# Cross attention followed by a maxout layer on one core: batch 0, W2·Wo and batch 1's attention in another written order

## The chip, the cores and the metric

One core of a Trainium2 chip runs the whole kernel. The metric is device time in microseconds (us) of one execution, the median of several. Engines: PE (TensorE, matrix products), DVE (VectorE), ACT (ScalarE), POOL (GpSimd) and SP (SyncE), which here issues all transfers.

## The reference

For each of 8 batches and 8 heads, `x` (512 tokens by 64) and a small `state` (32 by 64) attend to each other. The outputs, 544 rows a batch with the 8 heads side by side (512 columns), go through a layer that takes the maximum of two products.

```python
scores  = x @ state.T / 8;   a  = softmax(scores);   xread = a @ state     # 512 rows
scores2 = state @ x.T / 8;   a2 = softmax(scores2);  sread = a2 @ x        # 32 rows
h = concatenate([xread, sread])              # (8*544, 512)
out = maximum(h @ w1, h @ w2) @ w_out        # w1, w2: 512x1024, w_out: 1024x512
```

## The kernel before, in words

The maximum is rewritten: max(h w1, h w2) w_out = relu(h (w1 − w2)) w_out + h (w2 w_out). So the kernel needs `wd` = w1 − w2, `wo` = w_out in bf16 and `wwo` = w2·w_out, the last computed on PE (`w_wo`, line 422): 32 products of 512 columns from the transposed w2 (`w2t`, made in `w2_tr`, line 407) and `wo`. The weights come in four quarters of the 1024 hidden columns; each quarter is three transfers of 512 KB (`load_wq`, line 97) into staging tiles of which three of a kind exist.

For a batch `b`, xread = a·state is never formed. `sw` (line 304) multiplies `state` into the weights instead: SW[b] = state·wd (1024 columns) and state·wwo (512 columns). Layer 1 (`l1`, line 347) is relu(a·SW) in 8 pieces of two products, written to `r`. Layer 2 (`l2`, line 370) adds, for each of 4 tiles of 128 tokens, a·state·wwo (`l2_open`, line 356, two products from `aT`) and r·wo (`l2_f`, line 360, eight products). The attention of a batch is: cast x to bf16 (`xb`), transpose it (`xt`), scores and exp (`e`), row sums and division (`norm`, line 229, result `a`), transpose `a` (`aT`). The state's own read (`sread_mm`, line 256, called "the state read" below) multiplies `e` with x and, for the sums, with ones; from batch 2 on x and ones stand together in a tile `xo` of its own (`cast_x1`, line 144). Its result is scaled on DVE (`sread_norm`) and transposed (`sread_tr`); the 256 state rows of all batches go through the two layers at the end (`moe_sread`).

PSUM has eight banks, in two pools of four: `ps` for short products and `pa` (tile name `acc`) for layer 2 and the last chunk of `sw`. A pool hands its banks out in turn, so a product waits for the copy that empties the bank used four requests before.

The order of the work on each engine is the order in which the program is written (line 48, a manual schedule). Lines 446 to 555 are the first part: loads, batch 0, the four quarters of the weights, and the attention of batch 1. Batch 0 runs layer 2 in quarters as `wo` arrives (`l2_part`, line 439), keeping four `pa` banks open. Lines 558 to 590 are a loop over batches 1 to 7: layer 1, scores and division of the next batch, then the four tiles of layer 2 with `sw_all` and the state read of the next batch behind the second. `idle` (line 433) issues products on zeros. All transfers are on SP's one queue and are served in their order. Lines 58, 60 and 62 are the copy helpers on ACT, DVE and POOL.

Of the kernel before, what the change touches and what calls it, by code (L numbers as in the profile page):

```python
# [15 lines left out]
def kernel(  # L16
# [92 lines left out]
    def state0():  # L109
        nc.vector.tensor_copy(sb0, sf0)  # L110
# [5 lines left out]
        nc.vector.tensor_scalar(sbdn, sbd[:, 0], scalar1=-1.0, scalar2=None, op0=ALU.mult)  # L116
# [9 lines left out]
    def states():  # L126
        p = bank(BF16)
        for m in range(8):
            nc.tensor.transpose(p[:, m * 128:(m + 1) * 128], sbr[:, m].rearrange("p j d -> p (j d)"), ident)
        for j, e in ((0, "A"), (1, "V")):  # L130
            o = sbd[64 * j:64 * j + 64, 1:B, :, 32 * j:32 * j + 32].rearrange("p b k (l m) -> p (b k) l m", l=4)
            i = p[64 * j:64 * j + 64, :].rearrange("p (m k l) -> p k l m", m=8, l=4)[:, 4:]
            copy(e, o, i)


    def cast_x(b, engs):
        xb = xio.tile([128, NC, H * D], BF16, tag="xb", name="xb")
        for g in range(2):
            copy(engs[g],
                 xb[:, :, 256 * g:256 * g + 256].rearrange("p c (i d) -> p i c d", i=4),  # L140
                 xf_t[b][:, 4 * g:4 * g + 4, :].rearrange("p i (c d) -> p i c d", c=NC))
        st[b] = dict(xb=xb)

    def cast_x1(b):

        xo = stage.tile([128, NC, H, 66], BF16, tag="w1f", bufs=3, name="xo")
        nc.gpsimd.memset(xo[:, :, :, 64:65], 1.0)
        for g in range(2):
            nc.gpsimd.tensor_copy(xo[:, :, 4 * g:4 * g + 4, 0:D].rearrange("p c i d -> p i c d"),  # L149
                                  xf_t[b][:, 4 * g:4 * g + 4, :].rearrange("p i (c d) -> p i c d", c=NC))  # L150
        st[b]["xo"] = xo

    def cast_pair(b, k, eng):
        if k == 0:
            st[b] = dict(xb=xio.tile([128, NC, H * D], BF16, tag="xb", name="xb"))
        copy(eng, st[b]["xb"][:, :, 128 * k:128 * k + 128].rearrange("p c (i d) -> p i c d", i=2),
             xf_t[b][:, 2 * k:2 * k + 2, :].rearrange("p i (c d) -> p i c d", c=NC))

    def xt_pair(b, k, eng):
# [4 lines left out]
        for c in range(NC):  # L164
            nc.tensor.transpose(p[:, c * 128:(c + 1) * 128], d["xb"][:, c, k * 128:k * 128 + 128], ident)
# [48 lines left out]
    def scores(b, hh, pool=None):
        d = st[b]
        if hh == 0:
            att_tiles(b)
        p = bank(F32, pool)
# [6 lines left out]
        ev = d["e"].rearrange("p g c i n -> p (g c) i n")[:, :, 2 * hh:2 * hh + 2, :]  # L225
        nc.scalar.activation(out=ev.rearrange("p (g c) i n -> p g c (i n)", g=2),  # L226
                             in_=p.rearrange("p (c g m) -> p g c m", c=NC, g=2), func=ACTF.Exp, scale=scale)

    def norm(b, hh, eng):
# [16 lines left out]
    def at_pe(b, engs, pool=None):  # L246
        d = st[b]
        AT[b] = keep.tile([128, 2, NC, 128], BF16, tag="at", name="aT")
        for g in range(2):
            p = bank(BF16, pool)  # L250
            for c in range(NC):
                nc.tensor.transpose(p[:, c * 128:(c + 1) * 128],
                                    d["a"][:, g, c].rearrange("p i n -> p (i n)"), ident)
            copy(engs[g], AT[b][:, g].rearrange("p c t -> p (c t)"), p[:, 0:512])

    def sread_mm(b, pool=None):
# [15 lines left out]
        if "xo" not in d:
            for g in range(2):
                for c in range(NC):
                    nc.tensor.matmul(p[:, 256 + g:257 + g], d["e"][:, g, c].rearrange("p i n -> p (i n)"), ones[:, 0:1],
                                     start=False, stop=(c == NC - 1), skip_group_check=True)

    def sread_norm(b):
# [5 lines left out]
        if "xo" in d:  # L284
            pv = p[:, 0:260].rearrange("p (g i d) -> p g i d", g=2, i=2)
            nc.vector.reciprocal(rr, pv[:, :, 0, D])
            pv = pv[:, :, :, 0:D]
        else:
            nc.vector.reciprocal(rr, p[:, 256:258])
            pv = p[:, 0:256].rearrange("p (g i d) -> p g i d", g=2, i=2)  # L290
        for g in range(2):
            nc.vector.tensor_scalar(sr[:, :, g, :], pv[:, g], scalar1=rr[:, g:g + 1], scalar2=None, op0=ALU.mult)

    def sread_tr(b, eng, pool=None):
        d = st[b]
        p = bank(BF16, pool)
        for i in range(2):
            nc.tensor.transpose(p[:, i * 128:(i + 1) * 128], d["sr"][:, i].rearrange("p g d -> p (g d)"), ident)
        for i in range(2):
            copy(eng, sread_t.rearrange("p (a i) t -> p i a t", i=2)[:, i, :, b * Ns:(b + 1) * Ns],  # L300
                 p[:, i * 128:(i + 1) * 128].rearrange("p (a i n) -> p i a n", a=2, i=2)[:, i])


    def sw(b, lo, hi, engs=("V", "A"), pool=None):
        if b not in SW:
            SW[b] = big.tile([128, 2, WC], BF16, tag="sw", name="sw")
        pg = [bank(F32, pool), bank(F32, pool)]
        n = hi - lo
        for i in range(4):
            for g in range(2):  # L310
                rhs = wd[64 * g:64 * g + 64, i, lo:hi] if hi <= FF else wwo[64 * g:64 * g + 64, i, lo - FF:hi - FF]
                nc.tensor.matmul(pg[g][32 * i:32 * i + 32, 0:n],  # L312
                                 sbd[64 * g:64 * g + 64, b, i, 32 * g:32 * g + 32], rhs, start=True, stop=True)
        for g in range(2):
            copy(engs[g], SW[b][:, g, lo:hi], pg[g][:, 0:n])

    def sw_first(engs):

        SW[0] = big.tile([128, 2, WC], BF16, tag="sw", name="sw")
        pg = [bank(), bank()]  # L320
# [26 lines left out]
    def l1(b, f, eng=None):  # L347
        if f == 0:
            R[b] = big.tile([128, NF, NC * 128], BF16, tag="r", name="r")
        p = bank()  # L350
# [3 lines left out]
        relu(R[b][:, f, :], p, eng)  # L354
# [10 lines left out]
    def l2_out(b, c, p, eng):  # L365
        if c == 0:
# [36 lines left out]
    def w2_cast(q, eng):  # L403
        w2b[q] = stage.tile([128, 4, FQ], BF16, tag="w2b", bufs=2, name="w2b")
        copy(eng, w2b[q].rearrange("p i f -> p (i f)"), w2f[q].rearrange("p i f -> p (i f)"))

    def w2_tr(q, eng, pool=None):
        p = bank(BF16, pool)
# [4 lines left out]
        copy(eng, w2t[:, 2 * q:2 * q + 2].rearrange("p f i t -> p (f i t)"), p)  # L413
# [207 lines left out]
```

## Time and profile before

| | us |
|---|---|
| runs of the kernel | 165.0, 162.18, 163.86; median 163.86 |
| the profiled execution | 165.27 |
| its span, from the first to the last instruction | 163.6 |
| start of batch 1's layer 1 (end of the first part) | 50.34 |
| one batch in the loop (94.53 to 109.17) | 14.64 |

Over the span PE is busy 148.0 us, DVE 87.8, ACT 66.8 and POOL 54.6. The mean granted clock of PE is 0.986. Times in the rows are us from the span's start, unless they are marked ns. PE's "busy" counts overlapping products once, and the last product of a group shows some 0.2 us of its way through the array. PEld is the loading of weights.

### The profile page before, as it was taken

What the parts mean: (1) busy time and instruction counts of PE and PEld (TensorE: products, weight loads), DVE (VectorE), ACT (ScalarE), POOL (GpSimd) and SP (SyncE); (2) the same over time, 40 slices, a digit from 0 to 9 for tenths busy, and PEclk for the clock granted to TensorE, in tenths of its full rate; (3) what the DMA queues carried; (4) which work ended last, traced back from release to release, by engine and by line L of the source; (5) the groups of instructions that cost most, each with busy time, mean ns of one, the idle gap of its engine ahead of it and who ended that gap; (6) DMA issues with size and microseconds to landing.
All of it is one profiled execution on the core that took longest, in us unless ns stands there. A gap on an engine that the chain in (4) does not pass through costs nothing.

```text
span 163.6 us, 2847 instructions
## 1 busy us (share of the span) xinstructions
PE 148.0 (90%) x1142; PEld 71.7 (44%) x1142; DVE 87.8 (54%) x167; ACT 66.8 (41%) x131; POOL 54.6 (33%) x65
## 2 busy tenths in 40 slices
PE   5779989675999999998998999899999989999990
PEld 1436434453433544544453454345354534564430
DVE  3275756756867853654585457447554843731110
ACT  4234872544057450814454072537226451621000
POOL 1559455005940272263509225450900310000000
PEclk9999999998799999999999999999999999999998
DMA  3999999950234947798495858659523230601333
GB/s 93 271 373 360 363 360 356 353 187 2 52 76 192 196 72 251 257 132 214 170 284 101 262 212 176 146 174 311 104 38 160 96 67 1 256 0 36 98 128 128
DMA packets 34861, 29.09 MB, mean 178 GB/s; under 512 B 19872, under 2 KB 32160, under 8 KB 33952
## 3 DMA queue, kind: packets, MB, share of 16 engines
q1 hardware_dynamic: 34848, 28.91, 59.9%
q8 instruction: 9, 0.15, 0.4%
q14 instruction: 4, 0.03, 0.1%
HBM read 15.27 MB, written 8.91 MB: 148 GB/s over the span
## 4 chain that ended last, share of the span: by engine, by line
PE 71%; issue 12%; ACT 6%; DVE 3%; DMA 3%; SPq 1%; POOL 1%; POOLq 0%
PE acc L362 25%; PE ps L352 17%; PE acc L358 8%; PE ps L425 5%; DMA xf<-in_x_dram 3%; PE ps L268 2%; ACT ob L58 2%; PE ps L386 2%; PE acc L396 2%; ACT sw L58 2%; PE ps L223 2%; PE ps L411 2%; PE ps L312 1%; PE acc L394 1%; SPq L90 1%
## 5 line engine op out<-in xcount | busy, mean ns | idle before, releaser
L362 PE MATMUL acc<-wo,r 128*128 128x512 bf16 x256 | 60.5, 379 | 0.0
L362 PEld LDWEIGHTS <-r 128*128 128x128 bf16 x256 | 24.9, 98 | 29.5
L343 DVE TENSOR_SCALAR r<-ps 128x512 bf16<-128x512 f32 x32 | 22.1, 692 | 18.8 <-PE ps L352 18.7
L352 PE MATMUL ps<-aT,sw 128*128 128x512 bf16 x128 | 30.4, 387 | 1.2 <-DVE sw L60 1.2
L58 ACT COPY ob<-acc 128x512 f32<-128x512 f32 x16 | 9.4, 586 | 53.9 <-PE acc L362 36.0
L235 POOL TENSOR_TENSOR a<-e,er 128x512 bf16<-128x512 bf16 x14 | 14.4, 1051 | 47.4 <-DVE er L234 23.9
L341 ACT ACTIVATE r<-ps 128x512 bf16<-128x512 f32 x32 | 19.4, 605 | 11.2 <-PE ps L352 10.6
L62 POOL CAST xb<-xf 128x1024 bf16<-128x1024 f32 (+1 forms) x17 | 16.4, 974 | 21.3 <-DMA xf<-in_x_dram 21.2
L60 DVE COPY ob<-acc 128x512 f32<-128x512 f32 x16 | 10.7, 667 | 19.3 <-PE acc L362 18.9
L60 DVE CAST sw<-ps 128x512 bf16<-128x512 f32 (+1 forms) x20 | 12.0, 630 | 14.4 <-PE ps L312 12.9
L358 PE MATMUL acc<-sw,aT 128*128 128x512 bf16 x64 | 19.0, 380 | 0.3 <-DVE sw L60 0.3
L352 PEld LDWEIGHTS <-sw 128*128 128x128 bf16 x128 | 12.2, 98 | 15.2 <-DVE sw L60 1.4
L58 ACT CAST sw<-ps 128x512 bf16<-128x512 f32 (+1 forms) x20 | 10.3, 551 | 8.6 <-PE ps L312 7.3
L149 POOL CAST xo<-xf 128x1024 bf16<-128x1024 f32 x12 | 12.2, 1044 | 0.0
L233 DVE TENSOR_REDUCE es<-e 128x16 f32<-128x512 bf16 x14 | 9.2, 656 | 1.5 <-ACT e L226 1.5
L226 ACT ACTIVATE e<-ps 128x512 bf16<-128x512 f32 x14 | 7.6, 594 | 2.2 <-PE ps L223 1.6
L425 PE MATMUL ps<-wo,w2t 128*128 128x512 bf16 x32 | 8.3, 413 | 0.0
L358 PEld LDWEIGHTS <-aT 128*128 128x128 bf16 x64 | 5.2, 98 | 5.5 <-issue 0.9
L437 PE MATMUL acc<-wz 128*128 128x512 bf16 x13 | 6.4, 586 | 1.2 <-DVE ones L457 1.2
L268 PEld LDWEIGHTS <-e 128*64 128x64 bf16 x128 | 4.3, 116 | 5.9 <-ACT sw L58 5.5
L312 PE MATMUL ps<-wd,sbd 64*32 64x512 bf16 (+1 forms) x136 | 5.5, 364 | 1.4 <-DVE wd L416 1.4
L268 PE MATMUL ps<-xo,e 128*64 128x130 bf16 x96 | 4.0, 224 | 2.6 <-ACT sw L58 2.6
(93 smaller groups left out, 135.1 us busy)
## 6 DMA issues: line engine op xcount, KB each, us to landing
xf<-in_x_dram SPq DMA_DIRECT2D x14, 512.0 KB, 5.4
out_dram<-ob SPq DMA_DIRECT2D x7, 1024.0 KB, 4.4
w2f<-in_moe_w_dram SPq DMA_DIRECT2D x4, 512.0 KB, 9.2
w1f<-in_moe_w_dram SPq DMA_DIRECT2D x4, 512.0 KB, 9.8
wof<-in_moe_w_out_dram SPq DMA_DIRECT2D x4, 512.0 KB, 9.4
xf<-in_x_dram SPq DMA_DIRECT2D x4, 256.0 KB, 3.5
out_dram<-ob SPq DMA_DIRECT2D x2, 512.0 KB, 2.6
sfr<-in_state_dram SPq DMA_DIRECT2D x2, 256.0 KB, 8.6
```

The costliest lines, as they stand in the source:

```text
L58: nc.scalar.copy(o, i)
L60: nc.vector.tensor_copy(o, i)
L62: nc.gpsimd.tensor_copy(o, i)
L149: nc.gpsimd.tensor_copy(xo[:, :, 4 * g:4 * g + 4, 0:D].rearrange("p c i d -> p i c d"), xf_t[b][:, 4 * g:4 * g + 4, :].rearrange("p i (c d ...
L235: (nc.gpsimd if eng == "P" else nc.vector).tensor_mul(av, ev, d["er"][:, hh].unsqueeze(3).to_broadcast([128, 2 * NC, 2, Ns]))
L268: nc.tensor.matmul(p[64 * ih:64 * ih + 64, g * 2 * m:(g + 1) * 2 * m], d["e"][:, g, c, 2 * ih:2 * ih + 2].rearrange("p i n -> p (i n)"), x ...
L341: nc.scalar.activation(out=o, in_=p, func=ACTF.Relu)
L343: nc.vector.tensor_scalar(o, p, scalar1=0.0, scalar2=None, op0=ALU.max)
L352: nc.tensor.matmul(p, SW[b][:, g, f * 128:(f + 1) * 128], AT[b][:, g].rearrange("p c t -> p (c t)"), start=(g == 0), stop=(g == 1))
L358: nc.tensor.matmul(p, AT[b][:, g, c, :], SW[b][:, g, FF:WC], start=(start and g == 0), stop=(stop and g == 1))
L362: nc.tensor.matmul(p, R[b][:, f, c * 128:(c + 1) * 128], wo[:, f, :], start=(start and j == 0), stop=(stop and j == len(fs) - 1))
L425: nc.tensor.matmul(p, w2t[:, f, i, :], wo[:, f, :], start=(j == 0), stop=(j == len(fs) - 1))
```

## The change

The first part is written out anew. Its helpers are split into the products (`..._mm`) and the copy that empties the bank (`..._ev`), and 130 calls stand in a new order. W2·Wo is 16 pieces (a quarter, a block of rows) of two products; quarters 1 and 2, which shared a bank and one addition before, are now added one by one. x0 comes in two loads of 512 KB in place of four of 256 KB, the first ahead of state 0; all weights are loaded before x1. x0, and x1 too, are cast straight into the layout with ones (`xo`, now with the ones ahead of and behind each pair of heads), and the state read takes its operand from there. It takes its bank from `pa` in the loop. Some casts and differences change engine: w2's quarters 0 and 3 go from POOL to ACT, quarter 1 from ACT to POOL; w1 − w2 is on POOL for quarters 1 to 3 and on DVE for quarter 0, the reverse of before; w_out's quarter 1 goes from POOL to DVE, 2 from POOL to ACT, 3 from ACT to POOL.

```diff
+    load_x(0, 2, 0)
     load_state0()
-    load_x(0, 4)
-    for q in range(3):
-        load_wq(q)
+    load_x(0, 2, 1)
+    load_w2(0)
...
-    def cast_x1(b):
-        xo = stage.tile([128, NC, H, 66], BF16, tag="w1f", bufs=3, name="xo")
-        nc.gpsimd.memset(xo[:, :, :, 64:65], 1.0)
-        for g in range(2):
-            nc.gpsimd.tensor_copy(xo[:, :, 4 * g:4 * g + 4, 0:D].rearrange("p c i d -> p i c d"),
-                                  xf_t[b][:, 4 * g:4 * g + 4, :].rearrange("p i (c d) -> p i c d", c=NC))
+    def cast_xo(b):
+        alloc_x(b, "P", stage.tile([128, NC, 4, 132], BF16, tag="w1f", bufs=3, name="xo"))
+        for k in (0, 2):
+            cast_pair(b, k, "P", 2)
+    def alloc_x(b, eng, xo):
+        (nc.gpsimd if eng == "P" else nc.vector).memset(xo[:, :, :, 1:131:129], 1.0)
+        st.setdefault(b, {})["xo"] = xo
+    def cast_pair(b, k, eng, m=1):
+        xo = st[b]["xo"]
+        for j in range(k, k + m):
+            copy(eng, xo[:, :, j, 2:130].rearrange("p c (i d) -> p i c d", i=2),
+                 xf_t[b][:, 2 * j:2 * j + 2, :].rearrange("p i (c d) -> p i c d", c=NC))
...
     def sread_mm(b, pool=None):
-                                     xv[:, g, 2 * ih:2 * ih + 2],
+                                     d["xo"][:, c, 2 * ih:2 * ih + 2, 1 + 65 * g:66 + 65 * g],
...
-    def w_wo(fs, i, eng, first=False, last=False):
-        p = bank()
-        for j, f in enumerate(fs):
-            nc.tensor.matmul(p, w2t[:, f, i, :], wo[:, f, :], start=(j == 0), stop=(j == len(fs) - 1))
+    def w_wo_mm(q, i):
+        p = P["wwo", q, i] = bank()
+        for f in (2 * q, 2 * q + 1):
+            nc.tensor.matmul(p, w2t[:, f, i, :], wo[:, f, :], start=(f % 2 == 0), stop=(f % 2 == 1))
+    def w_wo_ev(q, i, eng):
+        if q == 0:
+            copy(eng, w2acc[:, i, :], P["wwo", q, i])
+        else:
+            nc.vector.tensor_tensor(wwo[:, i, :] if q == NQ - 1 else w2acc[:, i, :], P["wwo", q, i], w2acc[:, i, :],
+                                    op=ALU.add)
...
-    for i in range(4):
-        w_wo((2, 3, 4, 5), i, "V")
+    w_wo_mm(1, 1)
+    sread_tr_ev(0, "A")
...
             if n < B:
                 if c == 1:
                     sw_all(n)
-                    sread_mm(n)
+                    sread_mm(n, pa)
```

SP, the loads from quarter 2 on, before (`w2f`, `w1f`, `wof` are quarters of w2, w1 and w_out, `sfr` the states, `xf` an x):

```order
L100 DMA w2f<-in_moe_w_dram 128x4x256
L100 DMA w1f<-in_moe_w_dram 128x4x256
L102 DMA wof<-in_moe_w_out_dram 128x2x512
L121 DMA sfr<-in_state_dram 128x1x512 x2
L90 DMA xf<-in_x_dram 128x4x256 x2
L100 DMA w2f<-in_moe_w_dram 128x4x256
L100 DMA w1f<-in_moe_w_dram 128x4x256
L102 DMA wof<-in_moe_w_out_dram 128x2x512
L90 DMA xf<-in_x_dram 128x4x256 x4
```

The same place in the change:

```order
L101 DMA w1f<-in_moe_w_dram 128x4x256
L101 DMA w2f<-in_moe_w_dram 128x4x256
L108 DMA wof<-in_moe_w_out_dram 128x2x512
L101 DMA w2f<-in_moe_w_dram 128x4x256
L108 DMA wof<-in_moe_w_out_dram 128x2x512
L101 DMA w1f<-in_moe_w_dram 128x4x256
L91 DMA xf<-in_x_dram 128x4x256
L125 DMA sfr<-in_state_dram 128x1x512 x2
L91 DMA xf<-in_x_dram 128x4x256 x5
```

The fourth quarter moved ahead of x1 and the states. Its first load, of w2, reuses a staging tile and waits on SP for one of POOL's differences w1 − w2, as it did before: then for that of quarter 0, now for that of quarter 1.

DVE, before, from layer 1's first piece of batch 0 to the additions of W2·Wo's quarters 1 and 2 (`r` layer 1, `wd` a difference, `w2acc` the sum for W2·Wo):

```order
L343 TENSOR_SCALAR r<-ps 128x512
L289 RECIPROCAL rr<-acc 128x2
L292 TENSOR_SCALAR sr<-acc,rr 128x2x64 x2
L60 COPY w2acc<-ps 128x512 x2
L416 TENSOR_TENSOR wd<-w1f,w2f 128x4x256
L60 CAST sw<-ps 128x256
L343 TENSOR_SCALAR r<-ps 128x512
L416 TENSOR_TENSOR wd<-w1f,w2f 128x4x256
L60 CAST sw<-ps 128x256
L429 TENSOR_TENSOR w2acc<-ps,w2acc 128x512 x4
```

And in the change, from the state read's scaling of batch 0 on:

```order
L298 TENSOR_SCALAR sr<-acc,rr 128x2x64 x2
L448 TENSOR_TENSOR wd<-w1f,w2f 128x4x256
L60 COPY w2acc<-ps 128x512
L60 COPY w2t<-ps 128x1024
L60 CAST wo<-wof 128x1024
L463 TENSOR_TENSOR w2acc<-ps,w2acc 128x512 x3
L359 TENSOR_SCALAR r<-ps 128x512
L463 TENSOR_TENSOR w2acc<-ps,w2acc 128x512
L60 COPY w2t<-ps 128x1024
L60 CAST sw<-ps 128x256
L463 TENSOR_TENSOR w2acc<-ps,w2acc 128x512 x3
```

The additions of W2·Wo now stand among the other copies, there are 12 where there were 8, and one difference has gone to POOL while a cast of w_out has come.

PE in the loop, before, the end of `sw` and the beginning of the state read (`xo` is x with ones, `e` the exponentials):

```order
L312 MATMUL acc<-wwo,sbd 32x512
L312 LDWEIGHTS sbd
L312 MATMUL acc<-wwo,sbd 32x512
L268 LDWEIGHTS e
L268 MATMUL ps<-xo,e 64x130
```

And in the change:

```order
L322 MATMUL acc<-wwo,sbd 32x512
L322 LDWEIGHTS sbd
L322 MATMUL acc<-wwo,sbd 32x512
L283 LDWEIGHTS e
L283 MATMUL acc<-xo,e 64x130
```

Only the bank differs: the state read has left `ps` for `acc`.

## Rows read from the trace of the kernel before

**Rows 1.** Busy time by stretch: start:end, length, each engine's busy (instructions), PEclk, DMA share, GB/s.
```profile
0.00:17.37 17.37, 13.26 (x106) 6.91 (x107) 7.77 (x20) 6.56 (x13) 10.00 (x16) 1.00 0.86 279
17.37:34.88 17.51, 15.57 (x114) 7.74 (x113) 11.90 (x18) 10.24 (x16) 5.75 (x5) 1.00 1.07 351
34.88:43.69 8.81, 6.52 (x69) 3.43 (x68) 5.87 (x13) 2.99 (x5) 5.09 (x7) 0.81 0.04 13
43.69:50.34 6.65, 6.34 (x61) 2.42 (x60) 5.30 (x10) 3.18 (x7) 2.93 (x3) 1.00 0.42 81
94.53:109.17 14.64, 14.20 (x116) 6.72 (x114) 8.31 (x16) 6.25 (x14) 6.04 (x7) 1.00 0.72 198
```
**Rows 2.** The same view (PE, PEld, DVE, ACT, POOL), other stretches.
```profile
30.00:39.62 9.62, 5.84 (x92) 4.07 (x90) 6.69 (x11) 5.84 (x8) 1.02 (x2) 1.00 0.56 179
39.62:43.69 4.07, 4.07 (x11) 1.52 (x12) 2.12 (x6) 0.60 (x1) 4.07 (x7) 0.58 0.00 0
17.37:30.00 12.63, 12.19 (x82) 5.58 (x81) 8.96 (x15) 6.79 (x12) 5.75 (x5) 1.00 1.08 360
```
**Rows 3.** Timeline, PE: start, duration, line, operation, count, [idle before it <- releaser].
```profile
16.51 1.02 PE L352 MATMUL ps<-aT,sw 128*128 128x512 bf16 x4
...
26.04 3.63 PE L425 MATMUL ps<-wo,w2t 128*128 128x512 bf16 x16
...
32.91 0.62 PE L210 MATMUL ps<-ident,xb 128*128 128x128 bf16 x8 [1.49 <-ACT xb L58]
...
39.62 1.88 PE L352 MATMUL ps<-aT,sw 128*128 128x512 bf16 x4 [0.84 <-DVE sw L60]
...
41.29 2.78 PE L425 MATMUL ps<-wo,w2t 128*128 128x512 bf16 x8
```
**Rows 4.** Waits of PE over the span: total us, times, longest.
```profile
PE ps L268 <- ACT sw L58: 2.6, 6, 0.4
```
**Rows 5.** Timeline of one batch in the loop.
```profile
102.85 0.59 ACT L58 COPY ob<-acc 128x512 f32<-128x512 f32 x1 [3.45 <-issue]
103.14 0.40 PE L312 MATMUL acc<-wwo,sbd 64*32 64x512 bf16 x8
...
103.33 1.08 ACT L58 CAST sw<-ps 128x512 bf16<-128x512 f32 x2
...
103.98 0.66 PE L268 MATMUL ps<-xo,e 128*64 128x130 bf16 x16 [0.44 <-ACT sw L58]
...
107.74 0.61 DVE L292 TENSOR_SCALAR sr<-ps,rr 128x128 bf16<-128x128 f32 x2
...
108.69 0.31 PEld L298 LDWEIGHTS <-sr 128*128 128x128 bf16 x2
```
**Rows 6.** Timeline: one load's issue on SP and three casts that wait for loads.
```profile
17.86 1.70 SPq L100 DMA_DIRECT2D w2f<-in_moe_w_dram x1
...
21.94 1.04 POOL L62 CAST wo<-wof 128x1024 bf16<-128x1024 f32 x1 [3.49 <-DMA wof<-in_moe_w_out_dram]
...
24.82 1.58 POOL L62 CAST xb<-xf 128x1024 bf16<-128x1024 f32 x1 [0.40 <-DMA xf<-in_x_dram]
...
27.90 1.04 POOL L62 CAST w2b<-w2f 128x1024 bf16<-128x1024 f32 x1 [1.50 <-DMA w2f<-in_moe_w_dram]
```
**Rows 7.** Groups by form: count | busy us, mean ns of one | idle before.
```profile
L429 DVE TENSOR_TENSOR w2acc<-ps,w2acc 128x512 f32<-128x512 f32 x4 | 2.8, 692 | 1.1 <-PE ps L425 1.0
...
L416 POOL TENSOR_TENSOR wd<-w1f,w2f 128x1024 bf16<-128x1024 f32 x1 | 2.4, 2350 | 0.0
...
L286 DVE RECIPROCAL rr<-ps 128x2 f32<-128x2 f32 x6 | 1.0, 159 | 0.0
```
**Rows 8.** Timeline of POOL and DVE, batch 0's division among the casts of weights.
```profile
10.86 1.04 POOL L62 CAST w2b<-w2f 128x1024 bf16<-128x1024 f32 x1
...
11.22 0.96 DVE L194 TENSOR_TENSOR a<-e,er 128x256 bf16<-128x256 bf16 x1
...
12.61 1.03 POOL L62 CAST w1b<-w1f 128x1024 bf16<-128x1024 f32 x1
```

More of the change, by code (lines that the diff above doesn't have):

```diff
@@ L83, with load_x @@
     xf_t, st = {}, {}
-    def load_x(b, parts=2):
-        xf = xio.tile([128, H, NC * D], F32, tag="xf", name="xf")
-        xf_t[b] = xf
+    def load_x(b, parts=2, only=None):
+        if b not in xf_t:
+            xf_t[b] = xio.tile([128, H, NC * D], F32, tag="xf", name="xf")
+        xf = xf_t[b]
         m = H // parts
-        for g in range(parts):
+        for g in range(parts) if only is None else [only]:
             nc.sync.dma_start(
@@ L244, in at_dma, with at_mm, at_ev @@
                                     in_=d["a"].rearrange("p g c i n -> p (g c i n)"))
[L246 to L254, printed above, removed]
+    def at_mm(b, g):
+        if b not in AT:
+            AT[b] = keep.tile([128, 2, NC, 128], BF16, tag="at", name="aT")
+        p = P["at", g] = bank(BF16)
+        for c in range(NC):
+            nc.tensor.transpose(p[:, c * 128:(c + 1) * 128], st[b]["a"][:, g, c].rearrange("p i n -> p (i n)"), ident)
+    def at_ev(b, g, eng):
+        copy(eng, AT[b][:, g].rearrange("p c t -> p (c t)"), P["at", g][:, 0:512])
     def sread_mm(b, pool=None):
@@ L483 @@
-    norm_pair(0, 3, "V")
-    idle(2)
-    w2_tr(0, "A")
+    alloc_x(0, "P", big.tile([128, NC, 4, 132], BF16, tag="r", name="xo"))
+    idle(8)
+    cast_pair(0, 0, "V")
+    copy("V", sb0, sf0)
+    cast_pair(0, 1, "A")
+    idle(1)
+    xt_pair(0, 0, "V")
+    state0()
+    xt_pair(0, 1, "V")
+    nc.gpsimd.tensor_scalar(sbdn, sbd[:, 0], scalar1=-1.0, scalar2=None, op0=ALU.mult)
+    idle(1)
+    scores_pair(0, 0)
+    idle(1)
+    scores_pair(0, 1)
+    idle(1)
+    cast_pair(0, 2, "V")
+    cast_pair(0, 3, "P")
@@ L486 @@
+    idle(1)
+    reduce_pair(0, 0)
+    xt_pair(0, 2, "V")
+    reduce_pair(0, 1)
+    xt_pair(0, 3, "A")
+    norm(0, 0, "P", False)
+    idle(1)
+    scores_pair(0, 2)
+    scores_pair(0, 3)
+    idle(2)
+    w2_cast(0, "A")
+    reduce_pair(0, 2)
+    reduce_pair(0, 3)
+    norm(0, 1, "V", False)
+    w1_cast(("A", "P"))
     sread_mm(0, pa)
     idle(1)
+    w2_tr_mm(0)
+    w2_tr_ev(0, "V")
+    for g in range(2):
+        at_mm(0, g)
+        at_ev(0, g, "AV"[g])
     sw_first(("A", "V"))
-    at_pe(0, ("A", "V"))
@@ L511 @@
[L511 to L533 removed]
+    l1_mm(0, 0)
@@ new lines @@
+    l1_ev(0, 6, "A")
+    l2_part(2, 0)
+    xt_ev(1, 1, "V")
+    scores_mm(1, 0)
+    l1_ev(0, 7, "A")
+    w_wo_mm(3, 0)
+    scores_ev(1, 0)
+    cast_half(2, 1, "P")
+    xt_dma(2)
+    scores_mm(1, 1)
+    w_wo_ev(3, 0, "V")
+    l2_part(3, 2)
+    scores_ev(1, 1)
+    sw_mm(1, 0, 512)
+    norm_sums(1, 0)
+    l2_part(3, 0)
+    sw_ev(1, 0, 512, 0, "A")
+    sw_mm(0, FF, WC)
+    l2_part(3, 1)
+    sw_ev(1, 0, 512, 1, "V")
+    norm_mul(1, 0, "P")
+    sw_ev(0, FF, WC, 1, "A")
+    l2_part(3, 3)
```

395 lines of the change are left out of this document (225 added, 170 removed).

## Prediction

> **What bounds the kernel now.** I read the table of stretches first. From 50.34 us on the kernel repeats one pattern, and there PE is busy 14.20 of 14.64 us in a batch [rows 1]: PE bounds it, and what it does not use is one gap of 0.4 us. Before 50.34 it is different. The four stretches up to there hold 41.69 us of PE work in 50.34 us, and much of that "busy" time is matmuls at half speed [rows 1]. So this change, which rewrites everything up to 50.34, has a lot to win there and little behind it.
>
> Second, the same table cut where PE slows [rows 2]. From 17.37 to 30.00 PE is busy 12.19 of 12.63 us, a fill of 96.5%. From 30.00 to 39.62 it is busy 5.84 of 9.62 us. From 39.62 to 43.69 it is busy all the time, but the granted clock is 0.58: a mix of the two levels, mostly 1.2 GHz, after a stretch in which PE did little. What the gaps wait for stands in the order of time [rows 3]: the transposes of batch 1 wait 1.49 us for ACT's cast of x1 (32.91), and layer 1 waits 0.84 us for a copy on DVE (39.62). The 8 products of W2Wo at 41.29 then take 2.78 us, where 16 took 3.63 us at 26.04: 0.35 against 0.227 us each. Those waits are not for data that is late. They are for a cast or a copy that stands behind others in the written order, while PE's next independent work (W2Wo, layer 2) stands behind the waiting instruction.
>
> Third, the waits of PE: the only one that repeats is the state read (line 268), 2.6 us in 6 waits of 0.4 us, for a copy of `sw` on ACT [rows 4]. In one batch [rows 5]: PE ends the last `sw` product at about 103.54, ACT casts two `sw` tiles from 103.33, and the state read begins at 103.98. Its inputs have long been there; it waits for its bank of the pool `ps`, the four of which the `sw` products have just filled.
>
> **The change part by part.**
>
> *The state read in the other pool.* It moves to `pa`, where its bank was last used by an output tile of the same batch, copied out before the `sw` casts. So the 0.4 us goes, six times: 2.6 us, all on PE, which is the bound. What is late next: the output tile behind it needs a bank that ACT frees first of all (before both `sw` casts), and the one after has 2 us more. On DVE the read's scaling gains one reciprocal a batch, 0.16 us [rows 7]; the scaling ends at 108.35 and PE wants it at 108.69 [rows 5], so 0.34 us hides it. Bounds: 2.6 gained at best; at worst the wait comes back elsewhere and the gain is 0. The read's moving operand now begins at an odd element in half of its 16 products; no row shows such an operand. The nearest is today's 16 products in 0.66 us [rows 5]. Bounds: nothing, or twice that, 0.66 us in each of 7 reads (4.6 us). I take nothing, because 130 columns of the same strides are read. The cast into the new layout takes four POOL instructions of half size instead of two, some 0.4 us a batch on an engine that is busy 6.04 of 14.64 us [rows 1]: hidden.
>
> *The loads.* The last four landings of weights and x1 that POOL waits for are 21.94 (w_out, quarter 2, after 5.56 MB in the queue's order), 24.82 (first half of x1, 6.56 MB) and 27.90 (w2, quarter 3, 7.56 MB) [rows 6]: 2.98 us per MB, a saturated queue. With the new order w2's quarter 1 (3.06 MB) lands at 14.5, w1's quarter 1 (3.56) at 16.0, w2's quarter 3 (6.06) at 23.4 instead of 27.90, w1's quarter 3 (7.06) at 26.4, and x1's second half (8.56) at 30.9 instead of about 26.3. The total is the same; weights come 4.5 us earlier, x1 4.6 us later. One wait is added: the load of w2's quarter 3 needs a staging buffer that comes free with POOL's difference for quarter 1. It starts when w1's quarter 1 is there and takes 2.35 us [rows 7], so it ends at 18.4 to 19.4, and every later load stands behind it on SP. The two loads ahead of it keep the queue busy to 21.9, and in the trace the same load was issued at 17.86 to land 10 us later behind 3 MB of others [rows 6], so 2.5 us of lead should do. No gap, if POOL is not over 1 us late.
>
> *The start.* Today the casts of w2 and w1 are POOL's, one behind the other, with the w1 cast ending at 13.64 [rows 8], and layer 1 begins at 16.51 [rows 3]. In the change ACT casts w2, and ACT and POOL half of w1 each at its landing (11.6), so both end at about 12.3, 1.3 us earlier. The chain over x0 loses POOL's four casts in a row. I put layer 1 at 14.8; bounds 13.8 (all of it gained and more) and 16.5 (nothing). It matters little, since the next thing, the transposes of w2's quarter 1, needs POOL's cast of 1.04 us after 14.5. Two layer 1 pieces and three of W2Wo stand ahead of them: 10 products of 0.227 us, 2.3 us. So they begin at 17.05, bounds 15.7 and 18.5.
>
> *From there to batch 1's layer 1* (today at 50.34). PE still has to do: 26 products of W2Wo, 32 of layer 2 from `r`, 8 from `aT`, 12 of layer 1, 78 of 512 columns by 0.227 us [rows 3] = 17.7 us; 60 transposes of 128 columns, by columns 0.057 each = 3.4; four `sw` pieces of 0.40 [rows 5] and three half as wide at 0.3 = 2.5; 16 score products of 64 columns = 0.45; the state read 0.66. Together 24.7 us. The order puts one piece of W2Wo or layer 2 between any product and the copy it needs, so I take the fill of the well filled stretch, 96.5% [rows 2]: 25.6 us, and batch 1's layer 1 begins at 42.6 instead of 50.34, **7.7 us earlier**. Bounds: from 15.7 with no gap, 40.4; from 18.5 with the fill of 17.37 to 34.88 (15.57 of 17.51, 89%) [rows 1], 46.3. The change adds copies, since quarters 1 and 2 of W2Wo no longer add up in one bank: 16 evictions instead of 12, the four new ones additions on DVE of 0.69 us [rows 7], 2.8 us. DVE then has 23 instructions of 512 elements or as long, by 0.69, and some 5.8 us of others: 21.7 us of work in these 25.6. Hidden, but only just, and this is the weakest step. x1 must be there for its second half of transposes, which stand 9 us of PE work ahead of the end, at about 33: 30.9 and a cast of half of 1.04 us leave 1.5 us. The clock: no gap near those of 30 to 39.62 is left, so the 0.35 us products of 41.29 go too; that is inside the 7.7.
>
> *A lock between DVE and POOL.* DVE's multiplication at 11.22 takes 0.96 us and ends 0.28 us after POOL's cast (10.86 to 11.90) does [rows 8]: it stood still beside POOL. The Trainium skill ("SBUF — State Buffer", Who interferes with whom) states a lock that one of the two engines holds for a whole instruction, and counts not only DVE's instructions with two SBUF inputs but its fast casts from SBUF too. The row agrees for the first kind; no row shows the second, nor a cast of 1024 columns on DVE at all. I put that cast at POOL's 1.04 us [rows 8], bounds 0.69 (DVE's addition of 512 columns) and 2.35 (POOL's difference) [rows 7]. By the rule the cast of w_out's quarter 1, now on DVE, would stand behind POOL's 2.35 us difference, and one W2Wo piece would come 0.5 us later: 154.1 in place of 153.6. By the row alone, nothing. I take nothing: PE has other pieces until then.
>
> **Sum.** The profiled execution took 165.27 us, span 163.6. 165.27 − 7.7 − 2.6 = 155.0. The median of the three runs, 163.86, lies 1.41 lower, so the forecast is 153.6. The likeliest case's own range: 40.4 and 46.3 for the beginning of batch 1 give 151.3 and 157.2.
>
> **Rivals.**
> - *DVE and ACT become the bound of the first part.* For: 21.7 us of DVE work in 25.6, each piece of W2Wo holding one of four `ps` banks until DVE has added it. Against: DVE was busy 11.90 of 17.51 us beside an 89% fill. If PE is filled as over all of 17.37 to 50.34 (28.43 of 32.97, 86%) [rows 1], 24.7 us takes 28.7, batch 1 begins at 45.8: 156.7.
> - *The state read's wait is replaced* (another bank, the odd operand). For: `pa` also feeds layer 2. Against: the order of ACT's copies. Then only the 7.7 us stays: 156.2.
> - *The loads stall behind POOL.* If the quarter 1 difference ends 4 us late, x1 lands at 35, and with the cast and 9 us of PE work behind it batch 1 begins at 45: 156.0.
> - *Slower: the clock stays low.* Pieces that each wait a little might leave PE at 1.2 GHz up to batch 1, as after 39.62, where the clock was 0.58. The 24.7 us of work would double, batch 1 would begin at about 68, and the time would be 179. It is slower than today from the point where the loss exceeds 10.3 us, which is 45 of the 78 products at 0.454 instead of 0.227 us. Against: 17.37 to 34.88 ran at 1.00 [rows 1], with the same kinds of pieces.
>
> **How the numbers follow.** The forecast has 0.60; the first rival 0.18, the second 0.07, the third 0.05, all three still faster; two of them together, or a start that gains nothing, end around 159 to 162: 0.06; slower 0.04. This kernel's measurement can tell about 2% from no change (3.3 us: 160.6 and 167.1). Faster 0.90, within 2% 0.06, slower 0.04. The range reaches from the likeliest case's lower end to beyond the first three rivals: 150.8 to 158.5.
>
> **What would show it.** Batch 1's first layer 1 product at 41 to 45 us; the granted clock 1.00 from 17 to 50; PE's wait in the state read gone and the distance of batches at 14.25 in place of 14.64; POOL's quarter 1 difference ended before 20, and no hole in the DMA share before 35. I am wrong if the beginning of batch 1 lies after 46, if the batches keep 14.64 us, or if PE's waits move to DVE's additions.

## The result, and the profile after

The changed kernel takes **153.64 us** (median of 4 runs, 152.48 to 154.61) beside 164.13 us for the kernel before (4 runs, 162.18 to 165.0): a ratio of 0.9395, 95% interval 0.9262 to 0.9528. Faster, and at the forecast of 153.6. A few executions ran in a slower state; the ratios here and below leave them out, the medians do not. The profiled execution took 152.48 us with a span of 150.7 us, 12.9 us less than the span of 163.6 us before.

The table of stretches of the kernel after, with the columns of [rows 1]: the part up to batch 0's layer 2, the dense part, its end, all three together, and the first two batches of the loop.

```profile
0.00:16.38 16.38, 13.02 (x116) 6.92 (x119) 10.43 (x27) 8.83 (x17) 7.86 (x15) 1.00 0.90 297
16.38:30.00 13.62, 13.46 (x95) 6.25 (x96) 11.31 (x17) 8.69 (x18) 8.36 (x6) 1.00 1.03 348
30.00:40.52 10.52, 9.94 (x122) 5.10 (x122) 7.40 (x16) 7.63 (x15) 6.79 (x10) 1.00 0.84 194
0.00:40.52 40.52, 36.43 (x330) 18.28 (x335) 29.15 (x59) 25.15 (x48) 23.00 (x29) 1.00 0.93 287
40.52:54.71 14.19, 13.94 (x119) 6.71 (x115) 9.42 (x19) 6.40 (x12) 7.49 (x11) 1.00 0.91 205
54.71:68.90 14.19, 14.09 (x116) 6.79 (x116) 8.34 (x17) 6.25 (x13) 6.73 (x10) 1.00 0.86 205
```

Batch 1's layer 1 now begins at 40.52 instead of 50.34. Up to there PE did 36.43 us of work; before it did 41.69 us [rows 1]. Of the 9.82 us, 4.6 are gaps closed (8.65 us without PE work then, 4.09 now), and 5.3 are less PE time, among it the products at half speed at 41.29 [rows 3] and others in the start, shown below. The granted clock is 1.00 in each stretch, where 34.88 to 43.69 had 0.81 and 39.62 to 43.69, a part of it, 0.58 [rows 1, 2]. DVE in the second stretch is busy 83% of the time (11.31 of 13.62 us); e7 below loads it further.

PE's timeline of the kernel after: batch 0's layer 1, the transposes of w2's quarter 1, the transposes of batch 1 that waited before [rows 3] and its scores, and the first layer 1 products of batches 1, 2 and 7.

```profile
13.54 1.04 PE L368 MATMUL ps<-aT,sw 128*128 128x512 bf16 x4 [0.49 <-ACT sw L58]
...
15.71 0.61 PE L441 MATMUL ps<-ident,w2b 128*128 128x128 bf16 x8
...
29.95 0.61 PE L214 MATMUL ps<-ident,xo 128*128 128x128 bf16 x8
...
33.12 0.41 PE L228 MATMUL ps<-sbd,xt 128*128 128x64 bf16 x8 [0.37 <-DVE sbd L60]
...
40.52 3.68 PE L368 MATMUL ps<-aT,sw 128*128 128x512 bf16 x15
...
54.71 3.62 PE L368 MATMUL ps<-aT,sw 128*128 128x512 bf16 x16
...
125.39 3.62 PE L368 MATMUL ps<-aT,sw 128*128 128x512 bf16 x16
```

The waits of 1.49 and 0.84 us of [rows 3] are gone; the largest left between batch 0's layer 1 and batch 1's is 0.37 us. The batches stand 14.14 us apart ((125.39 − 54.71) / 5) instead of 14.64. One batch of the loop, in the timeline of the kernel after, for [rows 5]:

```profile
49.35 0.40 PE L322 MATMUL acc<-wwo,sbd 64*32 64x512 bf16 x8
...
49.49 1.08 ACT L58 CAST sw<-ps 128x512 bf16<-128x512 f32 x2
...
49.68 0.66 PE L283 MATMUL acc<-xo,e 128*64 128x130 bf16 x16
...
53.45 0.61 DVE L298 TENSOR_SCALAR sr<-acc,rr 128x128 bf16<-128x128 f32 x2
...
54.39 0.31 PEld L303 LDWEIGHTS <-sr 128*128 128x128 bf16 x2
```

The read now begins 0.33 us after the last eight `sw` products begin (49.35 to 49.68), where it began 0.84 us after that (103.14 to 103.98). It no longer waits for ACT's two casts, which still run (49.49 to 50.57). The read, half of whose products now begin at an odd element, takes 0.66 us, as before. The scaling on DVE ends at 54.06, 0.33 us before PE wants it, the margin of [rows 5].

So the span's 12.9 us come from three places: batch 0's layer 1 begins 2.97 us earlier (16.51 to 13.54), the stretch from there to batch 1's layer 1 is 6.85 us shorter (33.83 to 26.98), and six distances of batches give 3.08 us.

### The profile page after: what moved, and what is told of

It is laid out like the page before. It is cut to its first block, busy times and chain, and to the rows that moved or that the text cites. A ratio compares the mean times of both kernels' runs of the same rounds, so it can differ in the third digit from the quotient of the medians.

```text
span 150.7 us, 2837 instructions
## 1 busy us (share of the span) xinstructions
PE 141.3 (94%) x1110; PEld 69.5 (46%) x1130; DVE 86.8 (58%) x173; ACT 69.2 (46%) x139; POOL 57.9 (38%) x76
## 4 chain that ended last, share of the span: by engine, by line
PE 87%; DMA 3%; ACT 3%; issue 2%; DVE 1%; POOL 1%; SPq 0%
PE acc L384 37%; PE ps L368 18%; PE acc L380 9%; PE ps L457 5%; PE ps L322 4%; DMA sf<-in_state_dram 3%; PE acc L283 2%; PE ps L408 2%; PE acc L418 2%; PE ps L228 2%; PE ps L441 1%; PE acc L416 1%; DVE sbd L60 1%; PE acc L322 1%; ACT sbd L58 1%
## 5 line engine op out<-in xcount | busy, mean ns | idle before, releaser
L368 PE MATMUL ps<-aT,sw 128*128 128x512 bf16 x126 | 29.4, 379 | 0.6 <-ACT sw L58 0.5
L359 DVE TENSOR_SCALAR r<-ps 128x512 bf16<-128x512 f32 x30 | 20.7, 691 | 14.2 <-PE ps L368 14.1
L251 POOL TENSOR_TENSOR a<-e,er 128x512 bf16<-128x512 bf16 x15 | 15.5, 1048 | 33.2 <-ACT e L233 22.1
L357 ACT ACTIVATE r<-ps 128x512 bf16<-128x512 f32 x34 | 20.2, 604 | 5.4 <-PE ps L368 4.0
L60 DVE COPY ob<-acc 128x512 f32<-128x512 f32 x15 | 10.0, 668 | 16.7 <-PE acc L384 14.6
L62 POOL CAST xb<-xf 128x1024 bf16<-128x1024 f32 x12 | 12.4, 1040 | 14.8 <-DMA xf<-in_x_dram 14.8
L380 PE MATMUL acc<-sw,aT 128*128 128x512 bf16 x55 | 17.1, 381 | 0.3
L60 DVE CAST sw<-ps 128x512 bf16<-128x512 f32 (+1 forms) x16 | 10.1, 665 | 11.4 <-PE ps L322 11.4
L62 POOL CAST xo<-xf 128x512 bf16<-128x512 f32 x26 | 14.9, 614 | 0.9 <-DMA xf<-in_x_dram 0.5
L448 POOL TENSOR_TENSOR wd<-w1f,w2f 128x1024 bf16<-128x1024 f32 x3 | 7.6, 2535 | 3.1 <-DMA w2f<-in_moe_w_dram 1.8
L463 DVE TENSOR_TENSOR w2acc<-ps,w2acc 128x512 f32<-128x512 f32 x8 | 5.3, 688 | 1.7 <-PE ps L457 1.6
```

The source lines that it names most:

```text
L60: nc.vector.tensor_copy(o, i)
L62: nc.gpsimd.tensor_copy(o, i)
L357: nc.scalar.activation(out=o, in_=p, func=ACTF.Relu)
L359: nc.vector.tensor_scalar(o, p, scalar1=0.0, scalar2=None, op0=ALU.max)
L368: nc.tensor.matmul(p, SW[b][:, g, f * 128:(f + 1) * 128], AT[b][:, g].rearrange("p c t -> p (c t)"), start=(g == 0), stop=(g == 1))
L380: nc.tensor.matmul(p, AT[b][:, g, c, :], SW[b][:, g, FF:WC], start=(start and g == 0), stop=(stop and g == 1))
```

## The experiments

The times are medians, the ratios are against the kernel before on the same chip. In the text, "the stretch" is the time from batch 0's layer 1 to batch 1's layer 1 in the profiled execution. The unchanged kernel ran twice more in these sets: 152.82 us (ratio 0.9333, 0.9257 to 0.9409) and 152.62 us (0.9325, 0.9277 to 0.9373).

| kernel | us | ratio, 95% interval | layer 1 of batch 0 | stretch | batches apart |
|---|---|---|---|---|---|
| changed kernel | 153.64 | 0.9395, 0.9262 to 0.9528 | 13.54 | 26.98 | 14.14 |
| e1, read in `ps` | 155.91 | 0.9573, 0.9505 to 0.9640 | 13.72 | 27.11 | 14.64 |
| e2, before with read in `pa` | 160.31 | 0.9825, 0.9722 to 0.9928 | 17.25 | 33.88 | 14.14 |
| e3, old load order | 157.65 | 0.9683, 0.9614 to 0.9752 | 13.96 | 31.07 | |
| e4, before with new load order | 164.8 | 1.0123, 1.0055 to 1.0191 | 14.74 | 34.74 | |
| e5, x0 in quarters | 152.85 | 0.9333, 0.9250 to 0.9415 | 13.30 | 27.30 | |
| e6, three zero products | 152.63 | 0.9325, 0.9255 to 0.9395 | 13.66 | 26.97 | |
| e7, differences on DVE | 154.44 | 0.9429, 0.9359 to 0.9500 | 13.96 | 28.98 | |
| e8, unchanged | 152.82 | 0.9333, 0.9257 to 0.9409 | 14.68 | 26.96 | 14.14 |
| e10, first casts on POOL | 153.5 | 0.9389, 0.9314 to 0.9463 | 13.97 | 27.11 | |
| e12, unchanged | 152.62 | 0.9325, 0.9277 to 0.9373 | 13.26 | 27.11 | 14.14 |
| e9, split end | 152.29 | 0.9297, 0.9241 to 0.9353 | 14.93 | 26.97 | |
| e11, split end, state 0 first | 153.67 | 0.9352, 0.9279 to 0.9425 | 15.06 | 27.71 | |

**The state read, alone and undone.** In the loop of the changed kernel, and the reverse in the kernel before:

```diff
-                    sread_mm(n, pa)
+                    sread_mm(n)
```

> The changed kernel with the loop's state read back in the pool ps. Theory (the bank alone made the wait): the 0.4 us wait for ACT's copy of sw returns in six batches, the distance of batches goes from 14.14 back to 14.64 us, the time rises by 6 x 0.5 = 3.0 us to about 156.6; the first part still ends at 40.5. Rival (the new layout of x, or the shifted rotation of banks, removed the wait): 14.14 and 153.6 stay.

> The kernel before with nothing but the loop's state read moved to pa. Theory: the distance of batches falls to 14.14, 3.0 us less than before, 161.1. Rival (the move needs the other edits, or another wait takes its place): no change, 164.1.

The waits of PE over the span in e1:

```profile
PE ps L283 <- ACT sw L58: 2.6, 6, 0.4
```

With the read back in `ps`, the row of [rows 4] is back, word for word but for the line, and the distance of batches is 14.64 again. With the read in `pa`, the kernel before has 14.14 and a median 3.3 us under the 163.65 us that it has without the edit in that set; the interval of the ratio says 0.7 to 2.8% faster. (The layer 1 and the stretch of e2 in the table are from a profiled execution of 163.06 us, the longest of its four.) That is the loop's term, shown from both sides. It is 0.50 us a batch and not the 0.44 of the wait: the wait counts from the end of PE's last `sw` products, while without it the read also begins beside their last 0.07 us (0.40 us long, the read 0.33 us after their begin).

**The loads, in the old order under the new work, and the new order under the old work.**

```diff
 load_wo(2)
-load_w2(3)
-load_wo(3)
-load_w1(3)
-load_x(1, 2, 0)
 load_states()
+load_x(1, 2, 0)
 load_x(1, 2, 1)
+load_w2(3)
+load_w1(3)
+load_wo(3)
```

> The changed kernel with the old order of loads from w_out's quarter 2 on: states and x1 ahead of quarter 3. Theory (the written order was made for these landings and cannot give way): w2's quarter 3 lands some 4.4 us later, at 26.7 instead of 22.3; its cast on ACT ends at 27.7, PE stands before its transposes from about 25.3 to 27.8, and batch 1 begins 2.5 us later, at 43: 156.1. Rival (PE has enough other work, the order of loads is worth nothing): 153.6 to 154.1.

```diff
-    for q in range(3):
+    for q in range(4):
         load_wq(q)
...
     load_x(1)
-    load_wq(3)
```

> The kernel before with quarter 3 of the weights ahead of the states and x1, and nothing else. Theory (the loads win nothing without the new order of work): batch 1 begins at 50 to 52, the time is 164 to 165.5. Rival (the order of loads is where the first part's gain comes from): batch 1 begins 4 us or more earlier, 160 or less.

The timeline of e3 where PE stands, and PE's waits over its span:

```profile
25.41 0.59 PE L457 MATMUL ps<-wo,w2t 128*128 128x512 bf16 x2
27.13 1.04 ACT L58 CAST w2b<-w2f 128x1024 bf16<-128x1024 f32 x1 [3.79 <-DMA w2f<-in_moe_w_dram]
28.49 0.61 PE L441 MATMUL ps<-ident,w2b 128*128 128x128 bf16 x8 [2.49 <-ACT sw L58]
...
29.96 1.04 POOL L62 CAST wo<-wof 128x1024 bf16<-128x1024 f32 x1 [7.65 <-DMA wof<-in_moe_w_out_dram]
...
31.05 1.02 PE L457 MATMUL ps<-wo,w2t 128*128 128x512 bf16 x4 [0.65 <-POOL wo L62]
```
```profile
PE ps L441 <- ACT sw L58: 2.5, 1, 2.5
...
PE ps L457 <- POOL wo L62: 0.7, 1, 0.7
PE ps L322 <- POOL wd L448: 0.4, 1, 0.4
```

The order of work is fixed with the new landings in it. When w2's quarter 3 lands late, ACT stands 3.79 us before its cast, the `sw` casts behind it stand too, and PE behind those; the wait is put down to `sw`, but its origin is the landing in ACT's row. The stretch grows by 4.1 us (31.07 against 26.98), more than the 2.5 us expected: 2.49 us are this wait, and PE also waits 0.65 us for POOL's late cast of w_out and 0.42 us for POOL's difference behind it; the last 0.5 us shows no wait of its own and stays open. Under the old work the new order of loads gains nothing: the stretch is 0.9 us longer (34.74 against 33.83), and the interval of the ratio, 0.6 to 1.9% slower, lies above 1. Batch 1 began at 49.48, a little ahead of the 50 to 52 expected, because layer 1 of batch 0 came early in this execution (14.74). So neither half gives the whole: the new work with the old loads has 31.07 (−2.8 from 33.83), the new loads with the new work another −4.1.

**The start: x0's halves, the zero products, the engines of the first casts.**

```diff
-    load_x(0, 2, 0)
     load_state0()
-    load_x(0, 2, 1)
+    load_x(0, 4)
```

> The changed kernel with the old start of the loads: state 0 first, x0 in four loads of 256 KB. Theory (every landing moves with the start of the queue): layer 1 of batch 0 begins 1 to 1.5 us later than 13.5, POOL's cast of w2's quarter 1 at 14.5 instead of 13.3, and batch 1 about 1.2 us later, 41.7: 154.8. Rival (the start is hidden behind the weights): batch 1 at 40.5, 153.6.

```diff
-    idle(8)
+    idle(3)
```

> The changed kernel with three products on zeros at the start instead of eight. Theory (eight products in a row let PE run the first transposes and scores at full speed, 0.39 instead of 0.61 us for four transposes): these go back to 0.61 us, layer 1 of batch 0 begins 0.7 to 1.5 us later than 13.5 and batch 1 0.5 to 1 us later: 154.4. Rival (the speed of the start is hidden behind x0 and the weights): no change, 153.6.

```diff
-    w2_cast(0, "A")
+    w2_cast(0, "P")
...
-    w1_cast(("A", "P"))
+    w1_cast(("P", "P"))
```

> The changed kernel with the casts of w2's and w1's quarter 0 back on POOL, one behind the other. Theory (these engines, not the loads, made the start earlier, and a later start passes on whole): w1's cast ends 1 to 1.5 us later, batch 0's layer 1 begins at 14.6 to 15.5 and batch 1's 27 us behind it, 153.8 to 155. Rival (the start is hidden behind the weights): layer 1 later, batch 1 at 40.5 to 41 and the time unchanged.

The first two are misses: neither x0 in two loads nor the zero products are worth anything that a run shows. In e6 the first transposes and scores did go back to half speed, as its theory had it (eight transposes take 1.06 us at 8.07; the kernel after has 0.39 and 0.40 for four each), but they did so too in e8, which has all eight zero products, and layer 1, at 13.66, lies among the 13.26 to 14.68 of the unchanged kernel. The third misses in part: w1's cast ends 1.45 us later than in the unchanged kernel beside it (13.05 against 11.60), but layer 1 only 0.7 us (13.97 against 13.26), ahead of the 14.6 to 15.5 expected. The median is 0.9 us higher; the intervals overlap, and layer 1 of the unchanged kernel itself moves by 1.4 us between executions, so no run shows the 0.7 us for sure. The other 2 us or so of the start lie elsewhere, and a part shows when the traces of the old start are laid beside each other. PE in the profile of the kernel before:

```profile
11.96 1.04 PE L411 MATMUL ps<-ident,w2b 128*128 128x128 bf16 x8 [0.70 <-POOL w2b L62]
12.92 1.06 PE L268 MATMUL acc<-xb,e 128*64 128x128 bf16 x16
```

and in e4, whose start is written the same:

```profile
11.59 0.62 PE L411 MATMUL ps<-ident,w2b 128*128 128x128 bf16 x8 [0.55 <-POOL w2b L62]
12.14 0.64 PE L268 MATMUL acc<-xb,e 128*64 128x128 bf16 x16
...
14.74 1.02 PE L352 MATMUL ps<-aT,sw 128*128 128x512 bf16 x4
```

The same instructions take 1.04 and 1.06 us in the one and 0.62 and 0.64 in the other: PE stood at half speed in the first, though the granted clock reads 1.00 in both. POOL's cast of w1 ends at 13.64 and 13.27, nearly alike; layer 1 follows 2.87 us later in the first (16.51), with PE busy all the way, and 1.47 us later in the second (14.74). e2, the third trace of this start, is like the first (1.04, 1.06; 17.25). In the new order these transposes of w2's quarter 0 take 0.61 or 0.62 us in all eleven traces. So of the start's 2.97 us some 1.4 (2.87 − 1.47) go with the half-speed products of the profiled execution of the kernel before. Whether the written order decides that is open: one of the three traces of the old order is without them, and the two that have them are long executions of their kernels, 165.27 us where all runs span 162.09 to 165.35, and 163.06 where they span 159.22 to 163.06. The remaining 1.6 us are not taken apart. The w1 cast ends 1.7 us earlier (13.64 to 11.94), but e10 shows that such a delay does not pass on whole. What brings PE to full speed is open too: with five zero products less (e6) the transposes of w2 are as fast.

**Is DVE near its limit?** The last two differences of weights, w_sub(2) and w_sub(3), on DVE instead of POOL, 1.2 us each:

```diff
-    w_sub(2, 0, 4, "P")
+    w_sub(2, 0, 4, "V")
...
-    w_sub(3, 0, 4, "P")
+    w_sub(3, 0, 4, "V")
```

> The changed kernel with the differences w1 - w2 of quarters 2 and 3 on DVE at the same places of the order, 2.4 us more work for DVE and 4.7 us less for POOL. Theory (PE bounds the first part, DVE has some 4 us to spare): batch 1 begins at most 0.7 us later, 153.6 to 154.3. Rival (DVE bounds it): 2.4 us later, 156.0.

The timeline of e7:

```profile
21.34 1.23 DVE L448 TENSOR_TENSOR wd<-w1f,w2f 128x1024 bf16<-128x1024 f32 x1 [0.19 <-DMA w2f<-in_moe_w_dram]
...
22.92 0.61 PE L441 MATMUL ps<-ident,w2b 128*128 128x128 bf16 x8 [0.73 <-ACT r L357]
...
23.82 1.04 PE L384 MATMUL acc<-wo,r 128*128 128x512 bf16 x4 [0.30 <-DVE r L359]
```

The stretch is 2.0 us longer for 2.4 us of DVE work, where at most 0.7 was expected; the rival's 2.4 us is nearer. The theory that DVE has some 4 us to spare falls: the idle time is there (2.3 us in the dense part of the kernel after), but it did not take the first difference. From the transposes of w2's quarter 1 to those of quarter 3 the way is 1.5 us longer (11.07 against 9.57 us). A part of that is the wait for a landing (0.19 us here); the wait and the difference together hold up DVE's additions and `r` behind them, and PE behind those (0.73 and 0.30 us). The second difference waited for no load, and the way from there to layer 1 of batch 1 is 0.5 us longer for its 1.2 us of DVE work.

**The scatter, and a version with a split end.** e8 and e12 are the changed kernel once more.

> The changed kernel once more, unchanged. Theory (the scatter of some 2 us between executions lies in the landing of the first loads): the loop keeps 14.14 us a batch, and whatever the span differs by from 150.7 stands ahead of layer 1 of batch 0 (13.5 in the first trace). Rival (it lies in the loop or at the end): the first part ends at 40.5 again and the difference is behind it.

> The changed kernel, unchanged, as the reference of this set. Theory: the stretch from batch 0's first layer 1 product to batch 1's takes 27.0 us again (26.98 and 26.96 in two traces), the loop 14.14 us a batch, the time 152.5 to 154 according to the start. Rival: the stretch takes up a late start and is shorter when the start is later.

Their stretch is 26.96 and 27.11 us and their batches 14.14 us apart, while layer 1 begins at 14.68 and 13.26. So the scatter between executions lies ahead of layer 1, and passes on whole. Where it comes from shows in the start of the two, e8 first:

```profile
6.15 0.23 DVE L60 CAST sb<-sf 128x128 bf16<-128x128 f32 x1 [1.41 <-DMA sf<-in_state_dram]
...
8.24 1.04 PE L472 MATMUL acc<-wz 128*128 128x512 bf16 x2
```
```profile
5.22 0.23 DVE L60 CAST sb<-sf 128x128 bf16<-128x128 f32 x1 [0.41 <-DMA sf<-in_state_dram]
...
7.06 0.59 PE L472 MATMUL acc<-wz 128*128 128x512 bf16 x2
```

State 0 landed 0.9 us later in e8, as e8's theory has it, and so did x0's second half (its first cast begins at 8.29 against 7.41). PE's products (two on zeros in the second rows) also stayed at half speed up to about 10.9 in e8 and only to about 6 in e12; whether the other 0.5 us of the 1.42 is theirs is not shown. e9 copies the last output tile in halves by DVE and ACT and stores the last two tiles one by one; e11 also loads state 0 first.

```diff
+        if b == B - 1 and c == NC - 1:
+            copy("V", OB[b][:, c, 0:256], p[:, 0:256])
+            copy("A", OB[b][:, c, 256:512], p[:, 256:512])
+        else:
+            copy(eng, OB[b][:, c, :], p)
...
-            elif c % 2:
-                store(b, c - 1, c + 1)
+            elif c == 1:
+                store(b, 0, 2)
+            elif c > 1:
+                store(b, c, c + 1)
```

> The changed kernel with the last tile of the last batch copied in two halves by DVE and ACT, and the third and fourth tile stored by loads of 256 KB of their own instead of 512 KB together. Theory: 0.3 us from the copy and 0.3 to 0.4 from the shorter last transfer, 0.6 less than the unchanged kernel of the same set. Rival (the end is the fixed latency of a transfer, and one more in the queue costs as much): no change.

```diff
-    load_x(0, 2, 0)
     load_state0()
+    load_x(0, 2, 0)
```

> The same with state 0 loaded ahead of x0's first half. Theory (PE waits 0.6 to 0.8 us at the start for the cast of state 0, which lands at 5.9): state 0 lands near 3.1, layer 1 begins 0.2 to 0.5 us earlier, and so does batch 1. Rival (x0's first half lands as much later as the state's transfer took to issue, 0.7 us): no gain, or a loss of 0.3 us.

The end of e9 in its timeline:

```profile
147.74 0.42 DVE L60 COPY ob<-acc 128x256 f32<-128x256 f32 x1 [1.47 <-PE acc L384]
148.20 0.37 ACT L58 COPY ob<-acc 128x256 f32<-128x256 f32 x1 [4.15 <-DVE ob L60]
```

The halves did not run side by side: ACT's wait ends with DVE's half. From batch 1's layer 1 to the end e9 takes 109.8 us against 110.2, 0.3 to 0.4 of the 0.6 expected, and its median is 0.3 us below that of e12: inside both intervals, so no version here is shown to beat the changed kernel. e11 gave nothing: x0 then lands later, and PE waits 1.4 us for its cast. Its stretch of 27.71 us is taken up below, at the lock between DVE and POOL.

## Why the prediction was right, step by step

*The sum.* Made against the profiled execution it was 155.0, and the profiled execution took 152.48: the terms were 2.5 us too small together. That the median came out at 153.6 all the same is partly luck: the kernel before was profiled in an execution above its median, the changed one in the fastest of its four, and in the later sets the changed kernel runs at 152.6 to 152.8 beside 164.5 and 164.6 for the kernel before. The gain there is 11.7 and 12.0 us, where the sum had 10.3.

*The loop's term, 2.6 us.* Right in place, 0.5 us too small in size: 3.08 us measured, shown by e1 and e2. The row of waits left out the overlap of 0.07 us a batch. The bounds on the odd element and on the reciprocal close at nothing: 0.66 us as before, margin 0.33 us.

*"Batch 1's layer 1 at 42.6".* It was 40.52. The step that failed is the start: "I put layer 1 at 14.8 ... It matters little". Layer 1 began at 13.54, the transposes of w2's quarter 1 at 15.71 instead of 17.05, at the lower bound, and 1.34 of the 2.08 us are that. It matters as much as anything: the stretch behind it is 26.96 to 27.30 us in eight traces whose layer 1 begins anywhere from 13.26 to 14.93, so each microsecond there is one of the total (e11, with 27.71, is the exception). What I had not seen was that the profiled execution of the kernel before did its transposes of w2 and its read at half speed there; the granted clock of [rows 1] says 1.00. The fill was right: 24.02 of 24.81 us from the transposes of w2's quarter 1 at 15.71 to 40.52, 96.8% against the 96.5% taken. The work itself was some 0.7 us less than the 24.7 us counted.

*The landings.* All came 1.2 to 1.4 us before the forecast. The rows in the timeline of the kernel after that answer to [rows 6]:

```profile
17.68 0.37 SPq L101 DMA_DIRECT2D w2f<-in_moe_w_dram  x1
...
23.52 1.04 POOL L62 CAST wo<-wof 128x1024 bf16<-128x1024 f32 x1 [1.73 <-DMA wof<-in_moe_w_out_dram]
...
29.72 0.61 POOL L62 CAST xo<-xf 128x512 bf16<-128x512 f32 x1 [0.47 <-DMA xf<-in_x_dram]
```

The load of w2's quarter 3 was issued at 17.68, when POOL's difference had freed its buffer, earlier than the 18.4 to 19.4 forecast, and the DMA share shows no hole: 1.03 from 16.38 to 30.00 and 0.94 from 30 to 35. SP stood 4.4 us before this load. In the kernel before no such wait shows: the load was issued at 17.86 [rows 6], behind those of x1, when POOL's difference had ended at 17.13. The rival of stalled loads did not happen.

*The lock between DVE and POOL.* Priced at nothing, and in this execution the price was right, but not the doubt behind it. DVE and POOL in the kernel after, in order of time:

```profile
14.21 1.22 DVE L448 TENSOR_TENSOR wd<-w1f,w2f 128x1024 bf16<-128x1024 f32 x1
...
14.77 2.88 POOL L448 TENSOR_TENSOR wd<-w1f,w2f 128x1024 bf16<-128x1024 f32 x1 [0.47 <-DMA w1f<-in_moe_w_dram]
...
16.97 1.23 DVE L60 CAST wo<-wof 128x1024 bf16<-128x1024 f32 x1
```

DVE's cast began at 16.97 and ended at 18.20, 0.55 us after POOL's difference (17.65). In e5 it began at 16.73, took 1.58 us, and ended 0.56 us after POOL's; in e6 and e8, 0.55 and 0.56 after. A cast whose begin moves and whose end stays tied to POOL's stood still behind it. POOL's difference took 2.88 us beside DVE's own and 2.36 in the next quarter. By the rule of the Trainium skill ("SBUF — State Buffer", Who interferes with whom) this is so for DVE's fast casts from SBUF; the traces agree. PE had other pieces meanwhile: its next W2Wo products stand right behind layer 2's, with no wait. In e11 it was not so. There POOL's difference began ahead of DVE's:

```profile
15.39 2.35 POOL L452 TENSOR_TENSOR wd<-w1f,w2f 128x1024 bf16<-128x1024 f32 x1
15.73 3.09 DVE L452 TENSOR_TENSOR wd<-w1f,w2f 128x1024 bf16<-128x1024 f32 x1
...
19.94 0.68 DVE L60 CAST wo<-wof 128x1024 bf16<-128x1024 f32 x1
...
20.67 0.61 PE L461 MATMUL ps<-wo,w2t 128*128 128x512 bf16 x2 [0.56 <-DVE wo L60]
```

Behind both differences the same cast takes 0.68 us, so some 0.55 of its 1.23 us in the kernel after was standing still. DVE's difference took 3.09 us instead of 1.22, the cast came late, and PE waited 0.56 us for it; the stretch of e11 is 0.7 us longer than that of the kernel after. So a price of nothing holds where DVE's difference begins first (14.21 against 14.77 in the kernel after), which the prediction did not make a condition. In the other order e11 shows about the 0.5 us that the prediction gave by the rule, though by another step: there DVE's difference stood still and not its cast.

*The rivals.* That the read's wait is replaced: refuted, no wait of PE stands at line 283. That the clock stays low: refuted, 1.00 throughout from 16.38 on, and 16 products take 3.62 us at 54.71 as 16 took 3.63 at 26.04 in [rows 3]. That DVE and ACT bound the first part: it did not decide, but e7 shows it nearer than I thought; 1.2 us more on DVE costs 0.5 to 1.5 us, by its place.

## What to carry to other kernels

An early half-speed stretch is found by the duration of a known product and not by the column of the granted clock alone, so lay one shape's durations beside each other before a start is priced. A written order of work and the order of the loads are one thing: here, with the old loads, more than half of what the stretch had gained was gone (4.1 of 6.9 us), and with the new loads alone the stretch was 0.9 us longer. Where this kernel's stretch is filled to 97%, a late start ahead of it passed on whole. The removal of a wait that a row gave as 0.44 us was worth 0.50.

## What had not been expected of the hardware

The same eight transposes of the same program part took 1.04 us in the kernel before and 0.62 in e4, with the granted clock of that stretch (10 to 14 us) at 1.00 in both. DVE's and POOL's differences took 1.22 and 2.88 us where DVE's began first and 3.09 and 2.35 where POOL's did (e11). And the layer 1 of batch 0 of one and the same kernel begins between 13.26 and 14.68 us from execution to execution, while everything behind it repeats within 0.15 us.
